# Attention and a two-layer MLP: load order of the second batch, first-layer groups ahead of its turns, and the engine that casts Q and K

## The chip, the cores and the metric

The kernel runs on one core of a Trainium2 chip. Its engines work side by side, each from its own queue, in the order in which the queue was written: TensorE (PE; its weight loads are shown as PEld), VectorE (DVE), ScalarE (ACT), GpSimd (POOL) and SyncE (SP), which here only issues DMAs. The metric is the device time of one execution in microseconds (us), as the median of several runs.

## The reference: what is computed

Sliding-window attention over 8 batches, 8 heads, 576 positions and 64 values a head, with a window of 32 to each side, and behind it a two-layer MLP with a squared ReLU on the 4608 tokens of 512 values. All inputs and the output are float32.

```python
scores = scale * np.matmul(q, k.transpose(0, 1, 3, 2))
mask = np.abs(pos[:, None] - pos[None, :]) <= window        # window = 32
scores = np.where(mask, scores, -1000000000.0)
attn = np.exp(scores - max);  attn = attn / (sum + 1e-09)
x = np.matmul(attn, v)  ->  (4608, 512)
h = x @ w_in                       # 512 -> 2048
r = np.maximum(h, 0.0)
out = (s * (r * r) + b) @ w_out    # 2048 -> 512
```

## The kernel before

**Two programs in one.** Attention makes columns of XT (x transposed, bf16, a ring of 2048 tokens). The MLP reads them in token blocks of 224, 128, 160, 256, 256 and then 512 tokens. The first three blocks (512 tokens, NE = 3) come from batch 0 alone. `s1(m, f0)` is the first layer: for a block m it multiplies with 128 columns of w_in at a time (or two or four such, in the small blocks), four matmuls each, into one of the two halves of the PSUM tile W; ScalarE applies the ReLU (L1131), VectorE squares (L1133) into GT. `s2` is the second layer: 16 matmuls for each 128 tokens into a half of the tile O (L1142), scaled and given the bias on VectorE (L1158) and stored (L1162). For the first three blocks `early` (L1173) does the second layer instead: 128 tokens have four accumulators (both halves of O and of AVN), and it goes through w_out in eight steps, as the pieces of w_out come in. Ahead of it, `colsum` sums w_out by columns for the bias (L1183, L1187, L1190, L1192); it needs all pieces of w_out and uses the second half of AVN, which `early` can use only after that.

**Attention of batches 0 and 1.** Q and K of a pair of heads are loaded as 128 x 512 float32 (`load_pair`, L667), cast to bf16 (`cast_qk`, L692: K on VectorE; Q of batch 1 on GpSimd), transposed on TensorE into a half of W (L705) and copied out (L710, L711); this is called the turn of a pair (`turn_pair`). Scores (L944), exponentials (L987), masks (L992), the product with V (L869), the division (L893, L895) and a transpose (L902, L910) follow. The last 64 positions go by themselves (`load_rest`, `turn_rest`).

**Attention of batches 2 to 7.** `piece` loads 512 positions of Q, 512 of K, and the last 64 of both, in this order, as float32 into two neighbouring staging buffers (L752), casts them in two halves x = 0, 1 (L760) by the engines in CASTE (one pair of engines for batch 2, one for the later ones), and has the halves transposed by DMA (L767) into QT and KTR. GpSimd copies KTR to KT (L777). Scores are at L811, exponentials at L839, masks at L843. The loads of a batch wait for the product with V of two batches before (`paced`). V comes by L582 and is cast at L591.

**Staging.** All loads of weights and of Q and K share a ring of 8 buffers (STG), taken in the order in which the kernel's text asks for them. A load waits until the cast that read its buffer last is done. The casts write a ring of 6 buffers (NAT).

**Order.** The kernel's text adds tasks to a graph (`_Graph.add`) with a cost, a key and what they read and write. `plan` then lists them: at each step the task that can start first by its own clock, and among equals that with the lowest key. The list is the order of each engine's queue. For a DMA, `dma=("l", units, cost)` gives the time on the shared rings by units times cost in ns; `ORDER1` gives the order in which SyncE loads what follows w_in: ("w", i) is a quarter of w_out in two pieces (L554, cast at L557), ("p", i) the pair i of batch 1, ("v", i) a V tile of batch 1, ("e", 0) its last positions. `FIRST` lists what the kernel's text asks for between `colsum` and `early`: (m, i) is the i-th quarter of the first layer of block m, TURN the turn and the scores of the next pair of batch 1. As turns and first-layer groups both use the halves of W, whatever stands earlier in FIRST uses such a half first; between other tasks the planner is free.

The turns of batch 1 have key -17.5 and up, a first-layer group of the first blocks this one:

```python
key = P1[m, f0] if m >= NE else -20.0 + f0 // 4 + 0.1 * m
```

Of the kernel before, what the change touches and what calls it, by code (L numbers as in the profile page):

```python
# [30 lines left out]
WINE = ("pool", "pool", "pool", "pool")  # L31
TURNKEY = -17.5
TURN = (None, 0)
FIRST = ((0, 0), (0, 1), (1, 0), (1, 1), (2, 0), (0, 2), (2, 1), (1, 2), (2, 2), (0, 3), TURN, TURN, (1, 3), TURN, (2, 3), TURN)
WOUTE = (("pool", "pool"),) * 4
TAIL = ("act", "dve")
HOST = (("k", 3), ("q", 0))
HELD = (2200.0, 1500.0, 1500.0, 1500.0)
OPEN = -24.4
REST = ("pool", "pool")  # L40
ORDER1 = (("w", 0), ("w", 1), ("w", 2), ("w", 3), ("p", 0), ("p", 1), ("p", 2), ("p", 3),
          ("v", 0), ("v", 1), ("e", 0), ("v", 2), ("v", 3), ("v", 4))
SWITCH = 215.0
XTS = 4000.0
ROWS = 4
# [2 lines left out]
PACE = ((-1, -1, -1),) * 3  # L48
CASTS = 40.0
LATE = 8  # L50
CASTE = (("pool", "pool"), ("pool", "dve"))
SLACK = (1000.0, 2000.0, 3000.0, 3000.0)
PACEV = ((-1,-1,0,0,1),(0,0,1,1,2),(0,0,1,1,2))
EV0 = ("dve", "act", "dve", "act", "dve")
# [27 lines left out]
class _Graph:  # L82
# [13 lines left out]
    def add(self, stream, fns, cost, reads=(), writes=(), key=0.0, accum=False, dma=None, waits=(),  # L96
            lat=None, slack=0.0):
        if not isinstance(fns, list):
            fns = [fns]
        after = [self.chain] if key < -100 and self.chain else []  # L100
        t = _Task(len(self.tasks), stream, fns, cost, self.LAT[stream] if lat is None else lat, key,
                  dma, slack, after)
        t.deps.update(waits)
        for a in after:
            assert a.stream == stream
            a.next.append(t)
        for r in reads:
            assert r in self.writer, r
            t.deps.add(self.writer[r])
        for w in writes:  # L110
            if w in self.writer:
                t.deps.add(self.writer[w])
            if not accum:
                t.deps.update(self.readers.get(w, ()))
        t.deps.discard(t)
        for r in reads:
            self.readers.setdefault(r, []).append(t)
        for w in writes:
            self.writer[w] = t
            if not accum:  # L120
                self.readers[w] = []
        self.tasks.append(t)
        if key < -100:
            self.chain = t
        return t
# [201 lines left out]
def bass_sliding_window_symmetric__then__act_starrelu_kernel(  # L327
# [23 lines left out]
    with ExitStack() as es:  # L351
# [184 lines left out]
        def pieces(lo, hi, step):  # L536
            return range(lo // step, (hi - 1) // step + 1)

        def take(what, n):
            ring[what] += 1  # L540
            return (ring[what] - 1) % n
# [26 lines left out]
        def late(b):  # L568

            return "sp" if b < LATE else "act"  # L570
# [166 lines left out]
        def q_later(b):  # L737
            return QTS[b % 2].rearrange("p (i a) s -> p i a s", i=4)

        def piece(b, parts, key, waits):  # L740


            slot = b % 2
            ring["stg"] += ring["stg"] % 2
            ring["nat"] += ring["nat"] % 2
            si, _ = take("stg", NSTG), take("stg", NSTG)
            ni, _ = take("nat", NNAT), take("nat", NNAT)
            stg = STGS[:, si:si + 2, :].rearrange("p x c -> p (x c)")
            nat = NATS[:, ni:ni + 2, :].rearrange("p x c -> p (x c)")
            stgr, natr = [("STG", si), ("STG", si + 1)], [("NAT", ni), ("NAT", ni + 1)]  # L750
            top = max(p0 + n // 4 for _, _, n, p0 in parts)
            add(late(b), [lambda e, name=name, t0=t0, n=n, p0=p0: e.dma_start(  # L752
                stg[p0:p0 + n // 4, :].rearrange("p (h c) -> p h c", h=H),
                src_of[name][b, :, t0:t0 + n, :].rearrange("h (p i) d -> p h (i d)", i=4))
                for name, t0, n, p0 in parts],
                500.0 * len(parts), writes=stgr, key=key - 20.0, waits=waits,
                dma=("l", sum(n for _, _, n, _ in parts) // 8, 68.0 if late(b) == "sp" else 61.0))
            for x in (0, 1):
                eng = CASTE[min(b, 3) - 2][x]
                add(eng, lambda e, x=x: e.tensor_copy(  # L760
                    nat[0:top, 1024 * x:1024 * x + 1024].rearrange("p (i h d) -> p h i d", h=H, i=2),
                    stg[0:top, :].rearrange("p (h i d) -> p h i d", h=H, i=4)[:, :, 2 * x:2 * x + 2, :]),
                    110 + (0.53 if eng == "dve" else 1.05) * 1024, reads=stgr, writes=[("NAT", ni + x)], key=key + CASTS, slack=SLACK[0])
            for name, t0, n, p0 in parts:
                np_, s0, xs = n // 4, t0 // 4, pieces(t0, t0 + n, 64)
                dst = q_later(b)[:, :, :, 16 + s0:16 + s0 + np_] if name == "q" else KTR[slot][:, :, :, s0:s0 + np_]
                add("sp", lambda e, dst=dst, p0=p0, np_=np_: e.dma_start(  # L767
                    dst.rearrange("p i a s -> p (i a) s"), nat[p0:p0 + np_, :], transpose=True),
                    2000.0 if n > 64 else 1200.0, reads=natr,
                    writes=[("QT", slot, x, pr) for x in xs for pr in range(NPAIR)] if name == "q" else [("KTR", slot, t0)],  # L770
                    key=key + 0.1, dma=("t", np_, 20.0))
                if name == "q":
                    continue
                land["kt", b, t0] = g.tasks[-1]
                for c in range(t0, t0 + n, 128):
                    w = min(128, t0 + n - c)
                    add("pool", lambda e, c=c, w=w: e.tensor_copy(  # L777
                        KT[slot][:, :, c:c + w].rearrange("p a (s i) -> p a s i", i=4),
                        KTR[slot][:, :, :, c // 4:(c + w) // 4].rearrange("p i a s -> p a s i")),
                        100 + 5.5 * w, reads=[("KTR", slot, t0)],  # L780
                        writes=[("KT", slot, x, pr) for x in pieces(c, c + w, 64) for pr in range(NPAIR)],
                        key=key + 3.0, slack=SLACK[1])

        def later(b, key):
            slot = b % 2
            if b < 4:
                for c0, x in ((0, 0), (160, WIN + S)):
                    add("pool", lambda e, c0=c0: e.memset(QTS[slot][:, :, c0:c0 + 16], 0.0), 400,
                        writes=[("QTZ", slot, x)] + [("QT", slot, x, pr) for x in range(NTILE) for pr in range(NPAIR)],
                        key=key - 20.0)  # L790
            for i, parts in enumerate(((("q", 0, 512, 0),), (("k", 0, 512, 0),), (("q", 512, 64, 0), ("k", 512, 64, 32)))):
                piece(b, parts, key + 0.01 * i, [paced(b, PACE[min(b, 4) - 2][i])] +
                      ([land["v", seq_of(b - 1), group_of(b - 1)[-1]]] if b > PAIRS or LATE == PAIRS else []))
# [230 lines left out]
        def attention():  # L1024
# [30 lines left out]
            for i, src in enumerate((moe_s, moe_b)):  # L1055
# [3 lines left out]
                reads=[("SROW", 0), ("SROW", 1)], writes=[("SB128", 0), ("SB128", 1)], key=P2[0] - 8.0, slack=500.0)  # L1059
            for step in ORDER1:  # L1060
                if step[0] == "w":
# [119 lines left out]
        def colsum():  # L1181

            add("pe", [lambda e, fc=fc, x=x: e.matmul(  # L1183
                AVN[32 * x:32 * x + 32, 1, 0:128], lhsT=ONESW[:, 0:32], rhs=WOUT_BF[:, fc, 128 * x:128 * x + 128],
                start=(fc == 0), stop=(fc == 15)) for fc in range(16) for x in range(4)],
                1100, reads=["ONESW"] + [("Wout", i, x) for i in range(4) for x in (0, 1)], writes=[("AVN", 1)], key=-12.0)
            add("dve", [lambda e, x=x: e.tensor_copy(block[32 * x:32 * x + 32, 128 * x:128 * x + 128],  # L1187
                                                     AVN[32 * x:32 * x + 32, 1, 0:128]) for x in range(4)],
                800, reads=[("AVN", 1)], writes=[("OUTS", NOUT - 1)], key=-12.0)
            add("pe", lambda e: e.matmul(AVN[:, 1, :], lhsT=even, rhs=block, start=True, stop=True),  # L1190
                950, reads=[("OUTS", NOUT - 2), ("OUTS", NOUT - 1)], writes=[("AVN", 1)], key=-12.0)
            add("dve", lambda e: e.tensor_scalar(CVEC[:, :], AVN[:, 1, :], SB128[:, 1:2], None, ALU.mult),  # L1192
                680, reads=[("AVN", 1), ("SB128", 1)], writes=[("CVEC", x) for x in (0, 1)], key=P2[0])
# [9 lines left out]
        colsum()  # L1203
        for m, i in FIRST:
            if m is None:
# [269 lines left out]
```

## Time and profile before

| | us |
|---|---|
| median of 3 runs | 315.75 (314.89 to 316.14) |
| the profiled execution | 317.31 |
| its span, first to last instruction | 315.5 |
| TensorE busy | 296.7 |
| VectorE busy | 195.5 |
| GpSimd busy | 93.0 |
| GpSimd casts of later Q, K (L760) | 21, of 1271 ns on average |
| VectorE casts of later Q, K (L760) | 15, of 740 ns on average |
| queued DMA, share of 16 engines' span | 75.5% |

The profile is of one execution. A row of a timeline gives the start and the length in us, the engine, the line, the operation, what is written from what, and in brackets the idle time of the engine ahead of it and what ended that. Neighbouring instructions of one kind are merged (x8). A row of the DMA-issuing queue (SPq) has the time from issue to the end of issuing, waiting included. The matmuls of TensorE are pipelined, so their rows overlap a little.

### The profile page before, as it was taken

The page shows a single profiled execution, that of the slowest core. Times are in us where ns is not written, and L with a number is a line of the kernel's source. Part 1 is how long each engine was busy: PE and PEld are TensorE (multiplying, and loading weights), DVE is VectorE, ACT ScalarE, POOL GpSimd, SP SyncE. Part 2 cuts the span into 40 slices and gives each one's busy share as a digit, 9 for nine tenths or more (in the row PEclk, how much of TensorE's full clock was granted, in tenths as well). Part 3 has the DMA queues.
Part 4 walks back from the last instruction along what each step waited for, and adds up shares of the span by engine and source line. Part 5 has one row for each costly group of instructions (what it writes and reads, how often), then busy time and mean ns, then how long its engine had stood idle before and what let it go on. Part 6 is the DMA issues. An engine that isn't in the chain of part 4 may idle for free.

```text
span 315.5 us, 7901 instructions
## 1 busy us (share of the span) xinstructions
PE 296.7 (94%) x3304; PEld 160.6 (51%) x3348; DVE 195.5 (62%) x387; ACT 141.9 (45%) x224; POOL 93.0 (29%) x110
## 2 busy tenths in 40 slices
PE   7788989999979998999999999999999999999996
PEld 3367756577734544544444444444444444444444
DVE  4678476876596777888577687766445543333312
ACT  4755425356525773654255346444444333333300
POOL 5468854671236235131613241260000000000000
PEclk9999999999999999999999999999999999999999
DMA  6999999997998998799999999996221110000022
GB/s 198 331 386 386 372 251 218 218 199 246 236 188 205 294 140 166 219 225 169 175 318 157 161 221 336 165 154 162 64 59 50 52 46 33 35 34 34 36 91 80
DMA packets 100055, 56.10 MB, mean 178 GB/s; under 512 B 72048, under 2 KB 91248, under 8 KB 100016
## 3 DMA queue, kind: packets, MB, share of 16 engines
q1 hardware_dynamic: 100016, 55.56, 75.5%
q8 instruction: 27, 0.44, 0.6%
q14 instruction: 12, 0.10, 0.1%
HBM read 36.70 MB, written 9.44 MB: 146 GB/s over the span
## 4 chain that ended last, share of the span: by engine, by line
PE 68%; DMA 19%; DVE 6%; issue 3%; SPq 2%; POOL 1%; ACT 0%; POOLq 0%
PE o L1142 30%; PE w L1124 28%; DMA stg<-in_k_dram 10%; DMA stg<-in_moe_w_out_dram 3%; PE avn L869 3%; DMA stg<-in_moe_w_in_dram 3%; DVE gt L1133 2%; PE avn L1173 2%; DMA stg<-in_q_dram 2%; PE sc L811 1%; PE o L1173 1%; DMA vst<-in_v_dram 1%; SPq L667 1%; DVE xn L895 1%; DVE nat L760 1%
## 5 line engine op out<-in xcount | busy, mean ns | idle before, releaser
L1124 PE MATMUL w<-xt,win 128*128 128x512 bf16 (+4 forms) x749 | 140.2, 324 | 3.0 <-ACT r L1131 1.4
L1131 ACT ACTIVATE r<-w 128x512 bf16<-128x512 f32 (+2 forms) x148 | 86.6, 586 | 107.1 <-PE w L1124 91.3
L1142 PE MATMUL o<-wout,gt 128*128 128x512 bf16 (+1 forms) x510 | 123.1, 372 | 2.0 <-issue 1.4
L1133 DVE TENSOR_TENSOR gt<-r 128x512 bf16<-128x512 bf16 (+2 forms) x148 | 79.9, 545 | 72.3 <-ACT r L1131 71.9
L1124 PEld LDWEIGHTS w<-xt,win 128*128 128x128 bf16 x768 | 68.3, 98 | 54.0 <-DVE kt L711 0.9
L1142 PEld LDWEIGHTS o<-wout,gt 128*128 128x128 bf16 x528 | 50.6, 98 | 54.6
L760 POOL CAST nat<-stg 128x1024 bf16<-128x1024 f32 (+1 forms) x21 | 26.7, 1271 | 60.7 <-DMA stg<-in_q_dram 37.6
L777 POOL COPY kt<-ktr 128x512 bf16<-128x512 bf16 (+1 forms) x30 | 31.6, 1054 | 38.5 <-DMA ktr<-nat 37.1
L839 ACT ACTIVATE ex<-sc 128x1024 bf16<-128x1024 f32 (+1 forms) x28 | 28.7, 1023 | 23.2 <-PE avn L869 22.4
L1158 DVE SCALAR_TENSOR_TENSOR outs<-o,sb,cvec 128x512 f32<-128x512 f32 (+1 forms) x35 | 25.4, 729 | 14.2 <-PE o L1142 14.0
L895 DVE TENSOR_TENSOR xn<-avn,rec 128x512 bf16<-128x512 f32 (+1 forms) x31 | 21.4, 689 | 1.1 <-DVE rec L893 0.2
L843 DVE TENSOR_TENSOR ex<-ex,mask 128x1024 bf16<-128x1024 bf16 (+1 forms) x28 | 21.2, 758 | 1.0 <-ACT ex L839 0.2
L869 PE MATMUL avn<-vb,ex 64*64 64x65 bf16 x944 | 19.9, 197 | 1.5 <-issue 1.3
L869 PEld LDWEIGHTS avn<-vb,ex 64*64 64x64 bf16 x944 | 12.9, 106 | 14.5 <-issue 8.7
L760 DVE CAST nat<-stg 128x1024 bf16<-128x1024 f32 (+1 forms) x15 | 11.1, 740 | 7.2 <-DMA stg<-in_k_dram 5.1
L591 DVE CAST vb<-vst 128x512 bf16<-128x512 f32 (+1 forms) x28 | 13.7, 494 | 0.0
L811 PE MATMUL sc<-qt,kt 64*64 64x128 bf16 x432 | 11.3, 216 | 0.0
L910 ACT COPY xt<-avn 128x512 bf16<-128x512 bf16 (+2 forms) x14 | 7.1, 516 | 8.1 <-PE avn L902 8.1
L893 DVE RECIPROCAL rec<-avn 128x8 f32<-128x8 f32 (+1 forms) x31 | 6.2, 201 | 5.9 <-PE avn L869 5.5
L557 POOL CAST win<-stg 128x1024 bf16<-128x1024 f32 x8 | 8.4, 1056 | 3.7 <-DMA stg<-in_moe_w_in_dram 3.6
L557 POOL CAST wout<-stg 128x1024 bf16<-128x1024 f32 x8 | 9.0, 1122 | 1.7 <-DMA stg<-in_moe_w_out_dram 1.0
L1173 PE MATMUL o<-wout,gt 128*128 128x512 bf16 x29 | 8.2, 379 | 1.0 <-POOL wout L557 0.9
(119 smaller groups left out, 146.1 us busy)
## 6 DMA issues: line engine op xcount, KB each, us to landing
out_dram<-outs SPq DMA_DIRECT2D x35, 256.0 KB, 2.5
vst<-in_v_dram SPq DMA_DIRECT2D x28, 256.0 KB, 5.2
stg<-in_k_dram SPq DMA_DIRECT2D x6, 1024.0 KB, 11.1
stg<-in_q_dram SPq DMA_DIRECT2D x6, 1024.0 KB, 6.6
stg<-in_moe_w_in_dram SPq DMA_DIRECT2D x8, 512.0 KB, 9.2
stg<-in_moe_w_out_dram SPq DMA_DIRECT2D x8, 512.0 KB, 9.6
stg<-in_q_dram SPq DMA_DIRECT2D x8, 256.0 KB, 5.4
stg<-in_k_dram SPq DMA_DIRECT2D x8, 256.0 KB, 5.4
```

Of the source, the lines that this page charges most:

```text
L760: add(eng, lambda e, x=x: e.tensor_copy(nat[0:top, 1024 * x:1024 * x + 1024].rearrange("p (i h d) -> p h i d", h=H, i=2), stg[0:top, :].re ...
L777: add("pool", lambda e, c=c, w=w: e.tensor_copy(KT[slot][:, :, c:c + w].rearrange("p a (s i) -> p a s i", i=4), KTR[slot][:, :, :, c // 4: ...
L839: add("act", lambda e, dst=flat_dst, src=flat_src: e.activation(dst, src, AF.Exp, bias=0.0, scale=0.125), 190 + 0.833 * 512 * len(hs), rea ...
L843: add("dve", lambda e, flat=flat, mask=mask: e.tensor_tensor(flat, flat, mask, ALU.mult), 130 + 0.53 * 512 * len(hs), reads=[("E", ei, hp, ...
L869: return [lambda e: e.matmul(av[64 * x:64 * x + 64, h, 0:D + 1], lhsT=buf[64 * g:64 * g + 64, h % 2, h // 2, c:c + 64], rhs=VB[64 * g:64 * ...
L895: add("dve", lambda e: e.tensor_tensor(XN[xi][0:p1, :].rearrange("p (a c) -> p a c", a=H), av[0:p1, :, 0:D], REC[ri][0:p1, :].rearrange("p ...
L1124: add("pe", [lambda e, g=g, kc=kc: e.matmul(wt[:, g, :], lhsT=WIN_BF[:, kc, (f0 + g) * 128:(f0 + g + 1) * 128], rhs=XT[:, kc, t0 % XR:t0 % ...
L1131: add("act", lambda e: e.activation(rt, wt, AF.Relu, bias=0.0, scale=1.0), 190 + 0.833 * ng * nt, reads=[("W", wb)], writes=[("R1", rb)], ...
L1133: add("dve", lambda e: e.tensor_tensor(GT[gs][:, f0:f0 + ng, g0:g0 + nt], rt, rt, ALU.mult), 130 + 0.53 * ng * nt, reads=[("R1", rb)], wri ...
L1142: add("pe", [lambda e, fc=fc: e.matmul(O[:, ob, 0:cn], lhsT=GT[gs][:, fc, g0:g0 + 128], rhs=WOUT_BF[:, fc, c0:c0 + cn], start=(fc == 0), s ...
L1158: add("dve", lambda e: e.scalar_tensor_tensor(OUTS[us][:, 0:cn], bank, SB128[:, 0:1], CVEC[:, c0:c0 + cn], ALU.mult, ALU.add), 200 + 1.07 ...
L1173: add("pe", [lambda e, fc=fc, bank=bank, gs=gs, g0=g0: e.matmul(bank, lhsT=GT[gs][:, fc, g0:g0 + 128], rhs=WOUT_BF[:, fc, :], start=(fc == ...
```

## The change

Four constants change. The loads of batch 1 and w_out come in the order pairs 0 and 1, first half of w_out, pairs 2 and 3, second half of w_out (before: w_out, then the pairs). In FIRST, the last two first-layer groups stand ahead of all turns (before: between them). From batch 3 on, GpSimd casts both halves of each piece (before: the second half on VectorE). And the planner counts 74 instead of 68 ns a unit for loads of the later Q and K.

```diff
-FIRST = ((0, 0), (0, 1), (1, 0), (1, 1), (2, 0), (0, 2), (2, 1), (1, 2), (2, 2), (0, 3), TURN, TURN, (1, 3), TURN, (2, 3), TURN)
+FIRST = ((0, 0), (0, 1), (1, 0), (1, 1), (2, 0), (0, 2), (2, 1), (1, 2), (2, 2), (0, 3), (1, 3), (2, 3), TURN, TURN, TURN, TURN)
...
-ORDER1 = (("w", 0), ("w", 1), ("w", 2), ("w", 3), ("p", 0), ("p", 1), ("p", 2), ("p", 3),
-          ("v", 0), ("v", 1), ("e", 0), ("v", 2), ("v", 3), ("v", 4))
+ORDER1 = (("p", 0), ("p", 1), ("w", 0), ("w", 1), ("p", 2), ("p", 3), ("w", 2), ("w", 3), ("v", 0), ("v", 1), ("e", 0), ("v", 2), ("v", 3), ("v", 4))
...
-CASTE = (("pool", "pool"), ("pool", "dve"))
+CASTE = (("pool", "pool"), ("pool", "pool"))
...
                 500.0 * len(parts), writes=stgr, key=key - 20.0, waits=waits,
-                dma=("l", sum(n for _, _, n, _ in parts) // 8, 68.0 if late(b) == "sp" else 61.0))
+                dma=("l", sum(n for _, _, n, _ in parts) // 8, 74.0 if late(b) == "sp" else 61.0))
             for x in (0, 1):
                 eng = CASTE[min(b, 3) - 2][x]
                 add(eng, lambda e, x=x: e.tensor_copy(
...
```

## The prediction, made before the changed kernel was run

> **What bounds the kernel now.** I read the page's first lines, then the table of busy time by stretch, then TensorE's instructions in order of time with the idle time ahead of each, and last the other queues around its gaps.
>
> ```profile
> span 315.5 us, 7901 instructions
> PE 296.7 (94%) x3304; PEld 160.6 (51%) x3348; DVE 195.5 (62%) x387; ACT 141.9 (45%) x224; POOL 93.0 (29%) x110
> ...
> 20.00:30.00 10.00, 9.07 (x156) 7.98 (x156) 8.70 (x15) 6.18 (x12) 8.57 (x10) 1.00 1.05 386
> 30.00:40.00 10.00, 8.76 (x86) 6.89 (x88) 4.67 (x9) 3.94 (x8) 8.36 (x8) 1.00 1.07 372
> 40.00:50.00 10.00, 9.34 (x162) 6.36 (x164) 7.48 (x17) 3.73 (x7) 4.85 (x7) 1.00 1.02 232
> ...
> 80.00:90.00 10.00, 8.52 (x148) 5.77 (x148) 6.71 (x11) 4.88 (x8) 4.49 (x3) 1.00 1.16 224
> ...
> 100.00:120.00 20.00, 18.07 (x245) 9.34 (x240) 16.04 (x31) 14.14 (x23) 7.34 (x6) 1.00 1.04 230
> ...
> 220.00:260.00 40.00, 39.14 (x373) 18.82 (x377) 20.13 (x43) 16.33 (x26) 0.00 (x0) 1.00 0.19 56
> ```
>
> Columns after the stretch and its length are busy time of PE, PEld, DVE, ACT and POOL, then granted clock, DMA share and GB/s. TensorE is the bound: busy 296.7 of 315.5 us at full clock, and in the last third, where nothing else is scarce, 39.14 of 40. Its idle time is all that a change of order can win: 315.5 - 296.7 = 18.8 us, of which the ramp and the tail, which the change leaves alone, hold a good part. Between 20 and 120 us it gathers in few places: 30 to 40 (1.24 us), 80 to 90 (1.48), 100 to 120 (1.93). Four single gaps make most of it:
>
> ```profile
> 30.27 0.38 PE L1173 MATMUL o<-wout,gt 128*128 128x512 bf16 x1 [0.93 <-POOL wout L557]
> ...
> 40.24 0.40 PE L705 MATMUL w<-ident,nat 128*128 128x128 bf16 x4 [1.16 <-DVE nat L692]
> ...
> 88.77 0.32 PE L869 MATMUL avn<-vb,ex 64*64 64x65 bf16 x16 [1.27 <-issue]
> ...
> 119.42 0.40 PE L902 MATMUL avn<-ident,xn 128*128 128x128 bf16 x4 [1.30 <-DVE xn L895]
> ```
>
> 0.93 + 1.16 = 2.09 us come from the loads of w_out and of batch 1's heads; 1.27 + 1.30 = 2.57 us from something on VectorE. The ceiling of this change is thus near 4.7 us.
>
> **Part 1, the loads and the first-layer groups.** SyncE's queue serves loads in order, and DMA is full there (share 1.05 to 1.07), so I read landings from the casts that waited for them.
>
> ```profile
> 27.41 1.16 POOL L557 CAST win<-stg 128x1024 bf16<-128x1024 f32 x1 [0.31 <-DMA stg<-in_moe_w_in_dram]
> 28.76 3.78 POOL L557 CAST wout<-stg 128x1024 bf16<-128x1024 f32 x3 [0.18 <-DMA stg<-in_moe_w_out_dram]
> ...
> 38.19 1.04 POOL L557 CAST wout<-stg 128x1024 bf16<-128x1024 f32 x1 [0.31 <-DMA stg<-in_moe_w_out_dram]
> ...
> 40.38 0.62 POOL L692 CAST nat<-stg 128x512 bf16<-128x512 f32 x1 [0.48 <-DMA stg<-in_q_dram]
> ...
> 43.36 0.61 POOL L692 CAST nat<-stg 128x512 bf16<-128x512 f32 x1 [0.89 <-DMA stg<-in_q_dram]
> ```
>
> Eight w_out pieces land from 28.76 to 38.19, so 9.43 / 7 = 1.35 us each. From one Q of a pair to the Q two pairs on (40.38 to 43.36) four loads land: 0.75 us each. After the last w_in piece at 27.41 the new order then gives, as an estimate from these rows: pairs 0 and 1 by 30.4; four w_out pieces by 35.8; pairs 2 and 3 by 38.8; the last four w_out pieces by 44.2 instead of 38.2. The bytes are the same, and the loads of V behind them come when they did. The staging ring allows it: pairs 0 and 1 take buffers 0 to 3, the first w_out pieces 4 to 7, and pairs 2 and 3 come back to 0 to 3, which the casts of pairs 0 and 1 free at about 31, well ahead of their turn.
>
> ```profile
> 20.64 0.94 PE L1124 MATMUL w<-xt,win 128*128 128x224 bf16 x8
> ...
> 22.60 1.70 PE L1124 MATMUL w<-xt,win 128*128 128x224 bf16 x16
> ...
> 24.45 4.90 PE L1124 MATMUL w<-xt,win 128*128 128x224 bf16 x64
> ...
> 40.57 1.08 PE L1183 MATMUL avn<-wout,onesw 128*32 128x128 bf16 x64
> ...
> 46.84 0.81 PE L1173 MATMUL avn<-wout,gt 128*128 128x512 bf16 x3 [0.16 <-issue]
> ...
> 53.56 0.86 PE o L1173 x4
> ```
>
> What can TensorE do meanwhile? The twelve first-layer groups are 192 matmuls; 8 + 16 + 64 = 88 are done by 29.3. The 104 left, at 4.90 / 64 = 0.077 us each, are 8.0 us and need no load any more. They now stand ahead of the turns, so they fill 29.3 to 37.3, past the place where TensorE waited 0.93 us for w_out. At 37.3 the first half of w_out and pairs 0 and 1 are there: 24 second-layer matmuls into three banks, at 0.86 / 4 = 0.216 us each (the last row, from the chain that ended last), are 5.2 us, the turns and scores of four pairs some 3 us more, until about 45.5. The last w_out piece, cast for about 1.1 us, is ready at 45.3. So the 1.16 us wait for a turn also has cover, but with nothing to spare. What is late next: the column sum of w_out, at 40.57 before, needs all eight pieces, so it moves to about 45.5, and from it to the first use of the fourth bank it took 46.84 - 40.57 = 6.27 us; that bank opens at about 51.8 instead. Until then the second half of w_out gives three banks another 5.2 us of work, plus the last scores. That is cover to about 51, a microsecond short.
>
> Bounds: all of 2.09 us won; or, if the last w_out pieces come into an empty queue and the column sum holds its bank back, some 2 us lost. I take 1.2 us won: two waits gone, less the microsecond by which the cover is short.
>
> **Part 2, the casts.** Fifteen halves go from VectorE to GpSimd.
>
> ```profile
> L760 POOL CAST nat<-stg x21: 1032/1210/1578, 57.4 to 200.0; 128x1024 bf16<-128x1024 f32 x14, 48x1024 bf16<-48x1024 f32 x7
> L760 DVE CAST nat<-stg x15: 676/685/1519, 81.2 to 201.5; 128x1024 bf16<-128x1024 f32 x10, 48x1024 bf16<-48x1024 f32 x5
> ...
> 83.99 0.69 DVE L895 TENSOR_TENSOR xn<-avn,rec 128x512 bf16<-128x512 f32 x1
> 86.53 0.69 DVE L760 CAST nat<-stg 128x1024 bf16<-128x1024 f32 x1 [1.85 <-DMA stg<-in_k_dram]
> 87.14 1.52 DVE L843 TENSOR_TENSOR ex<-ex,mask 128x1024 bf16<-128x1024 bf16 x1
> ...
> 108.89 0.69 DVE L760 CAST nat<-stg 128x1024 bf16<-128x1024 f32 x1 [1.12 <-DMA stg<-in_q_dram]
> ...
> 112.45 0.42 DVE L1133 TENSOR_TENSOR gt<-r 128x512 bf16<-128x512 bf16 x1
> 114.55 0.69 DVE L760 CAST nat<-stg 128x1024 bf16<-128x1024 f32 x1 [1.69 <-DMA stg<-in_k_dram]
> 115.16 1.26 DVE L1133 TENSOR_TENSOR gt<-r 128x512 bf16<-128x512 bf16 x1
> 116.34 1.52 DVE L760 CAST nat<-stg 48x1024 bf16<-48x1024 f32 x1
> ...
> 118.67 0.69 DVE L895 TENSOR_TENSOR xn<-avn,rec 128x512 bf16<-128x512 f32 x1
> ```
>
> This is what the two gaps of 2.57 us are. VectorE's queue is in order. At 84.7 it stands at the cast of a K load that lands at 86.5; the mask of the exponentials behind it then runs until 88.66, and TensorE starts the product with V at 88.77. At 112.9 the same: it waits 1.69 us for K, casts twice, and the normalised rows that TensorE waits for end at 119.36. With no cast of a load on VectorE these waits stand on GpSimd, where only casts and K copies are queued. Gain: 2.57 less the 0.16 us that such a change of operands shows anyway (the 46.84 row), twice: 2.25 us. Bounds: 2.57, and nothing.
>
> The cost: GpSimd does both halves in turn, at 1.21 us (median) for the second one, 15 x 1.21 = 18 us on an engine busy 93.0 of 315.5. Behind the casts stand the transposes in SyncE's queue and the K copies.
>
> ```profile
> 82.13 5.22 SPq L1162 DMA_DIRECT2D out_dram<-outs  x1
> ...
> 89.08 2.91 SPq L767 DMA_TRANSPOSE qt<-nat  x1
> 92.10 3.04 SPq L767 DMA_TRANSPOSE ktr<-nat  x1
> ...
> 97.54 5.69 POOL L777 COPY kt<-ktr 128x512 bf16<-128x512 bf16 x5 [7.97 <-DMA ktr<-nat]
> ...
> 99.75 0.24 PE L811 MATMUL sc<-qt,kt 64*64 64x128 bf16 x1
> ...
> 56.50:65.00 8.50, 8.05 (x163) 5.11 (x163) 7.08 (x15) 2.57 (x5) 7.03 (x8) 1.00 1.07 231
> ```
>
> For batch 3, K lands at 86.5, two GpSimd casts end by 89.0, and its transpose left at 92.10 anyway, because SyncE stood 5.22 us at a store that VectorE owed. So the later half costs nothing as long as SyncE is the later one; without that cover it is 1.21 us for each of five batches, against a margin of 99.75 - (97.54 + 5.69 / 5) = 1.07 us. Batch 2 already casts everything on GpSimd, and in its stretch (56.5 to 65) TensorE idles 0.45 us of 8.5.
>
> What speaks against it stands in the same rows: a square that takes 0.42 us alone takes 1.26 at 115.16, beside a GpSimd cast. One more such delay per moved cast is 15 x 0.84 = 12.6 us on VectorE, more than the 15 x 0.685 = 10.3 us taken from it. I still count it as nothing, since four buffers lie between squares and their readers, but it is a rival below.
>
> The Trainium skill ("SBUF — State Buffer", Who interferes with whom) says that a VectorE instruction with two SBUF inputs and a GpSimd one that reads SBUF exclude one another for a whole instruction. The 1.26 us row agrees. By that rule alone the sum would have no VectorE gain in it and would come to rival C.
>
> **Part 3, the planner's 74 for 68.** It moves no instruction by itself; the planned landing of a full piece (64 units) comes 64 x 6 = 384 ns later, so casts, transposes and scores are placed behind more MLP work. Q landed at 108.9 and K at 114.55, 5.6 us for one piece, so later is nearer to the truth. Counted at nothing: TensorE has MLP work to put first until the end. Were a score to come so late that a block's rows are missing, the cost is at most 0.4 us a piece.
>
> **Sum.** -1.2 - 2.25 = -3.45 us. The profiled execution took 317.31 us (span 315.5), 1.56 above the median of 315.75; it becomes 313.86, and the median 312.3.
>
> **Rivals.** A is the forecast, 312.3 (its own range 310.9 to 313.9).
> B: the loads win nothing, because the column sum and the last w_out pieces take the waits over. For it: the cover above ends a microsecond short. Against: 8.0 us of groups free of loads. Casts alone: 315.75 - 2.25 = 313.5.
> C: the casts win nothing: GpSimd's second cast holds VectorE by 0.84 us where it stood for a load before, so masks and normalised rows come as late. For: the 1.26 and 1.52 us rows. Against: batch 2's stretch. 315.75 - 1.2 = 314.55. The same time comes out if the planner puts new waits where the old ones were.
> D, slower: K arrives late. GpSimd's two extra casts of K and of the short piece (2 x 1.21 = 2.42 us) both come before the first K copy, and TensorE's score stands in order ahead of MLP work. Price: (2.42 - 1.07) x 5 batches = 6.8 us; with the gains, 315.75 + 6.8 - 3.45 = 319.1. It decides from a lateness of 1.07 + 3.45 / 5 = 1.76 us a batch on. Against: SyncE's cover of 3 us, and a planner that knows of the longer cast and puts the scores later.
>
> **Chances.** A 0.48, B 0.15, C 0.20, D 0.17. Half a per cent, 1.6 us, is about what can be told from no change: faster (below 314.2) is A and most of B, 0.60; no change is C with the edges of the others, 0.22; slower (above 317.3) 0.18. The range reaches down to all of 4.7 us and a little of the smaller waits, 310.4, and up to a D that is two thirds paid, 318.0.
>
> **What would show it.** Right: first-layer groups dense from 29 to 37 us with no wait for w_out; no VectorE cast behind a K load after 60 us; no gap over 0.5 us at 80 to 90 and 100 to 120; idle in 20 to 120 us down by some 3.5. Wrong: a wait for w_out or for the column sum's bank between 42 and 52; scores (L811) preceded by idle time that ends with GpSimd's K copy; squares of 1.26 us ahead of every TensorE gap; or a TensorE that is late at 220 us by as much as it is at the end.

## The result, and the profile after

| | before | after |
|---|---|---|
| median of 22 runs each, us | 315.02 | 313.36 |
| lowest and highest | 313.77 to 318.06 | 312.42 to 317.73 |
| ratio after / before, 95% interval | | 0.994 (0.9919 to 0.996) |
| the profiled execution | 317.31 | 312.42 |

The change wins 0.6%, some 1.9 us. Ratios here leave disturbed executions out; the medians beside them do not. The two profiled executions differ by 4.9 us, far more: the one of before is among its slowest, the one of after its fastest. So these two traces show where waits stood, but not what they are worth in the median; that took more traces of before.

The page of the changed kernel, then its table of busy time by stretch (columns as before):

```profile
span 310.6 us, 7883 instructions
PE 295.3 (95%) x3305; PEld 160.3 (52%) x3348; DVE 191.8 (62%) x372; ACT 142.3 (46%) x224; POOL 106.8 (34%) x125
...
L1132 DVE TENSOR_TENSOR gt<-r 128x512 bf16<-128x512 bf16 (+2 forms) x148 | 87.1, 601 | 69.2 <-ACT r L1130 68.5
...
L759 POOL CAST nat<-stg 128x1024 bf16<-128x1024 f32 (+1 forms) x36 | 41.1, 1140 | 51.2 <-DMA stg<-in_q_dram 38.2
```

```profile
20.00:30.00 10.00, 9.80 (x156) 9.10 (x156) 6.24 (x15) 6.60 (x13) 6.59 (x7) 1.00 1.06 374
30.00:40.00 10.00, 9.42 (x108) 7.74 (x108) 6.14 (x11) 4.66 (x11) 6.80 (x8) 1.00 1.07 374
40.00:50.00 10.00, 9.25 (x160) 5.35 (x159) 8.94 (x18) 5.11 (x8) 7.23 (x9) 1.00 1.04 251
...
80.00:90.00 10.00, 9.79 (x150) 5.89 (x151) 6.95 (x12) 4.95 (x7) 5.70 (x6) 1.00 1.23 204
...
100.00:120.00 20.00, 19.33 (x228) 9.78 (x230) 17.01 (x30) 11.74 (x20) 9.33 (x9) 1.00 1.06 206
```

(Line numbers are one lower from here on, as the diff takes a line out.) TensorE's idle time fell from 0.93 to 0.20 us at 20 to 30, from 1.24 to 0.58 at 30 to 40, from 1.48 to 0.21 at 80 to 90 and from 1.93 to 0.67 at 100 to 120. It grew a little at 40 to 50 (0.66 to 0.75). Some of this idle time is not real, and the last section comes back to it. All four gaps that the prediction named are gone, and two smaller ones have come. GpSimd's 36 casts took 41.1 us, at a mean of 1140 ns (1271 before). TensorE's timeline of after:

```profile
23.87 7.92 PE L1123 MATMUL w<-xt,win 128*128 128x224 bf16 x104
32.28 0.38 PE L1172 MATMUL o<-wout,gt 128*128 128x512 bf16 x1 [0.48 <-POOL wout L556]
...
44.48 1.08 PE L1182 MATMUL avn<-wout,onesw 128*32 128x128 bf16 x64 [0.53 <-POOL wout L556]
```

The first-layer groups do run on without a load: 104 matmuls in one piece where before there were 64. But the planner still asked for w_out in the middle of them, 0.48 us early, and for the column sum ahead of the last w_out cast, 0.53 us early. GpSimd's queue gives the landings that the prediction had worked out:

```profile
30.96 1.04 POOL L556 CAST wout<-stg 128x1024 bf16<-128x1024 f32 x1 [3.20 <-DMA stg<-in_moe_w_out_dram]
...
35.15 1.04 POOL L556 CAST wout<-stg 128x1024 bf16<-128x1024 f32 x1 [0.52 <-DMA stg<-in_moe_w_out_dram]
...
39.29 1.06 POOL L556 CAST wout<-stg 128x1024 bf16<-128x1024 f32 x1 [0.99 <-DMA stg<-in_moe_w_out_dram]
...
43.39 1.04 POOL L556 CAST wout<-stg 128x1024 bf16<-128x1024 f32 x1 [0.25 <-DMA stg<-in_moe_w_out_dram]
```

The fourth piece starts its cast at 35.15 (35.8 was estimated for its landing), the last at 43.39 (44.2).

**Three stretches.** To compare traces whose start-up differs by up to 1.2 us, I cut each at three of TensorE's rows: the first first-layer group, the first group of block 3 (which needs batch 1), and the last merged run of the second layer. For before and after:

```profile
61.94 1.92 PE L1124 MATMUL w<-xt,win 128*128 128x256 bf16 x16
...
297.50 14.88 PE L1142 MATMUL o<-wout,gt 128*128 128x512 bf16 x83
```

```profile
20.20 0.94 PE L1123 MATMUL w<-xt,win 128*128 128x224 bf16 x8
...
59.93 1.92 PE L1123 MATMUL w<-xt,win 128*128 128x256 bf16 x16
...
292.64 14.88 PE L1141 MATMUL o<-wout,gt 128*128 128x512 bf16 x83
```

Early: 61.94 - 20.64 = 41.30 us before, 59.93 - 20.20 = 39.73 after. Middle: 297.50 - 61.94 = 235.56 before, 232.71 after. The rest, 18.00 and 17.96, is the same in all traces to 0.4 us. The experiments below are read by these two numbers beside their times.

### The profile page after: what moved, and what is told of

The parts are those of the page before. It is cut to its first block, busy times and chain, and to the rows that moved or that the text cites. A ratio compares the mean times of both kernels' runs of the same rounds, so it can differ in the third digit from the quotient of the medians.

```text
span 310.6 us, 7883 instructions
## 1 busy us (share of the span) xinstructions
PE 295.3 (95%) x3305; PEld 160.3 (52%) x3348; DVE 191.8 (62%) x372; ACT 142.3 (46%) x224; POOL 106.8 (34%) x125
## 4 chain that ended last, share of the span: by engine, by line
PE 78%; DMA 12%; SPq 3%; issue 2%; POOL 2%; DVE 2%; ACT 0%; POOLq 0%
PE o L1141 35%; PE w L1123 32%; DMA stg<-in_moe_w_out_dram 5%; PE avn L868 4%; DMA stg<-in_moe_w_in_dram 3%; DMA stg<-in_k_dram 3%; PE sc L810 2%; PE avn L1172 2%; DMA stg<-in_v_dram 1%; DVE gt L1132 1%; SPq L666 1%; PE o L1172 1%; POOL wout L556 1%; SPq L677 1%; PE avn L901 1%
## 5 line engine op out<-in xcount | busy, mean ns | idle before, releaser
L1123 PE MATMUL w<-xt,win 128*128 128x512 bf16 (+4 forms) x750 | 138.2, 325 | 2.9 <-ACT r L1130 1.6
L1132 DVE TENSOR_TENSOR gt<-r 128x512 bf16<-128x512 bf16 (+2 forms) x148 | 87.1, 601 | 69.2 <-ACT r L1130 68.5
L1141 PE MATMUL o<-wout,gt 128*128 128x512 bf16 (+1 forms) x508 | 120.6, 372 | 2.4 <-issue 1.6
L759 POOL CAST nat<-stg 128x1024 bf16<-128x1024 f32 (+1 forms) x36 | 41.1, 1140 | 51.2 <-DMA stg<-in_q_dram 38.2
L776 POOL COPY kt<-ktr 128x512 bf16<-128x512 bf16 (+1 forms) x30 | 30.8, 1028 | 36.0 <-DMA ktr<-nat 34.5
L842 DVE TENSOR_TENSOR ex<-ex,mask 128x1024 bf16<-128x1024 bf16 (+1 forms) x28 | 19.8, 708 | 1.2 <-ACT ex L838 0.5
L590 DVE CAST vb<-vst 128x512 bf16<-128x512 f32 (+1 forms) x28 | 12.3, 445 | 1.1 <-DMA vst<-in_v_dram 1.1
L986 ACT ACTIVATE ex<-sc 128x1024 bf16<-128x1024 f32 (+2 forms) x7 | 6.2, 902 | 5.0 <-PE sc L943 5.0
## 6 DMA issues: line engine op xcount, KB each, us to landing
stg<-in_k_dram SPq DMA_DIRECT2D x6, 1024.0 KB, 10.4
```

Of the source, the lines that this page charges most:

```text
L759: add(eng, lambda e, x=x: e.tensor_copy(nat[0:top, 1024 * x:1024 * x + 1024].rearrange("p (i h d) -> p h i d", h=H, i=2), stg[0:top, :].re ...
L776: add("pool", lambda e, c=c, w=w: e.tensor_copy(KT[slot][:, :, c:c + w].rearrange("p a (s i) -> p a s i", i=4), KTR[slot][:, :, :, c // 4: ...
L842: add("dve", lambda e, flat=flat, mask=mask: e.tensor_tensor(flat, flat, mask, ALU.mult), 130 + 0.53 * 512 * len(hs), reads=[("E", ei, hp, ...
L1123: add("pe", [lambda e, g=g, kc=kc: e.matmul(wt[:, g, :], lhsT=WIN_BF[:, kc, (f0 + g) * 128:(f0 + g + 1) * 128], rhs=XT[:, kc, t0 % XR:t0 % ...
L1132: add("dve", lambda e: e.tensor_tensor(GT[gs][:, f0:f0 + ng, g0:g0 + nt], rt, rt, ALU.mult), 130 + 0.53 * ng * nt, reads=[("R1", rb)], wri ...
L1141: add("pe", [lambda e, fc=fc: e.matmul(O[:, ob, 0:cn], lhsT=GT[gs][:, fc, g0:g0 + 128], rhs=WOUT_BF[:, fc, c0:c0 + cn], start=(fc == 0), s ...
```

## The experiments

| run | loads | groups | casts | cost | ratio (95%) | traced, us | early | middle |
|---|---|---|---|---|---|---|---|---|
| first trace of before | old | old | old | 68 | | 317.31 | 41.30 | 235.56 |
| c1_before_again | old | old | old | 68 | | 316.16 | 41.17 | 233.89 |
| c3_before_third | old | old | old | 68 | | 314.47 | 41.10 | 232.84 |
| c4_before_fourth | old | old | old | 68 | | 317.08 | 41.07 | 235.67 |
| e1_loads | new | new | old | 68 | 1.0009 (0.9978 to 1.0041) | 319.02 | 40.66 | 237.20 |
| e2_casts | old | old | new | 68 | 0.9999 (0.9964 to 1.0034) | 318.18 | 41.16 | 236.44 |
| e3_cost | old | old | old | 74 | 1.0 (0.9976 to 1.0023) | 314.93 | 40.34 | 233.35 |
| e4_loads_casts | new | new | new | 68 | 0.9969 (0.9938 to 1.0001) | 314.61 | 40.23 | 233.61 |
| e5_loads_cost | new | new | old | 74 | 0.9958 (0.9931 to 0.9984) | 313.8 | 40.01 | 233.07 |
| e6_casts_cost | old | old | new | 74 | 0.9992 (0.9968 to 1.0016) | 314.36 | 41.04 | 233.20 |
| e7_order_casts_cost | new | old | new | 74 | 1.0007 (0.9983 to 1.0031) | 316.3 | 42.86 | 232.57 |
| the change, first trace | new | new | new | 74 | 0.994 (0.9919 to 0.996) | 312.42 | 39.73 | 232.71 |
| c2_after_again | new | new | new | 74 | 0.994 (0.9914 to 0.9966) | 314.43 | 40.82 | 232.78 |
| e8_held | new | new | new | 74 | 0.9982 (0.9941 to 1.0023) | 312.81 | 39.97 | 232.75 |

The table has all eight combinations of three parts: loads and groups, casts, cost. With the old loads and groups, nothing moves the ratio: 0.9999, 1.0 and 0.9992 for casts, cost and both. With the new ones it is 1.0009 alone, 0.9969 with the casts, 0.9958 with the cost and 0.994 with both. So the loads win only together with another part, and the other parts only together with the loads. Neighbours among these four have intervals that overlap; those of the first and the last lie apart.

The middle stretch sorts by the cost: 232.57 to 233.35 us in the seven traces with 74, 232.84 to 237.20 in the seven with 68. The third trace of before is thus as short there as those of the changed kernel. The sizes are those of single executions: three of the seven with 74 are the fastest of their kernel (the first of the change, e6, e8).

### The kernel before, three more times

No edit.

> The kernel before, unchanged, for a second trace. The first one belongs to an execution of 317.31 us, while the median of all is 315.02. If the four gaps are a fixed consequence of the written order, they are here again, each within 0.3 us (0.93, 1.16, 1.27, 1.30), and the 2.3 us of difference lie elsewhere. If they depend on when loads happen to land, at least one of the two VectorE gaps (1.27, 1.30) is below 0.6 us here, and the changed kernel can win less from them in the median than the first trace showed.

> The kernel before, a third trace. The forecast's sum took 2.57 us for two VectorE gaps out of a trace of 317.31 us; the second trace (316.16 us) had one of 0.98. Theory G (these gaps belong to slower executions, where K lands later against VectorE's queue): in an execution near the median of 315.4 or below, they sum to under 1 us. Rival: they sum to 1 us or more whatever the time.

> As the run ahead of it, a fourth trace: by theory G the time above 313.5 us of span goes with the sum of the VectorE gaps; by the rival the gaps are of one size and the times differ by the start, the granted clock or gaps elsewhere.

The two early gaps came back each time. In the order of the runs, TensorE's gaps over 0.3 us from 29 us on:

```profile
31.00 0.38 PE L1173 MATMUL o<-wout,gt 128*128 128x512 bf16 x1 [1.05 <-POOL wout L557]
41.01 0.40 PE L705 MATMUL w<-ident,nat 128*128 128x128 bf16 x4 [1.21 <-DVE nat L692]
89.09 0.32 PE L869 MATMUL avn<-vb,ex 64*64 64x65 bf16 x16 [0.98 <-issue]
```

```profile
29.77 0.60 PE L1173 MATMUL o<-wout,gt 128*128 128x512 bf16 x2 [0.53 <-POOL wout L557]
40.04 0.40 PE L705 MATMUL w<-ident,nat 128*128 128x128 bf16 x4 [1.24 <-DVE nat L692]
```

```profile
29.91 0.60 PE L1173 MATMUL o<-wout,gt 128*128 128x512 bf16 x2 [0.64 <-POOL wout L557]
40.12 0.40 PE L705 MATMUL w<-ident,nat 128*128 128x128 bf16 x4 [1.18 <-DVE nat L692]
88.13 0.32 PE L869 MATMUL avn<-vb,ex 64*64 64x65 bf16 x16 [0.81 <-issue]
102.11 0.34 PE L902 MATMUL avn<-ident,xn 96*128 96x96 bf16 x4 [0.53 <-DVE xn L895]
143.88 0.32 PE L869 MATMUL avn<-vb,ex 64*64 64x65 bf16 x16 [1.38 <-DVE ex L843]
```

The 0.53 us in the fourth trace has another cause. No cast of a load stands ahead of it; two squares do, which took 2.29 us beside GpSimd's K copies (0.42 us is one square alone):

```profile
98.92 2.29 DVE L1133 TENSOR_TENSOR gt<-r 128x512 bf16<-128x512 bf16 x2 [0.74 <-ACT r L1131]
```

```profile
96.37 5.32 POOL L777 COPY kt<-ktr 128x512 bf16<-128x512 bf16 x5 [7.44 <-DMA ktr<-nat]
```

With the first trace, the gaps behind VectorE's waits for loads sum to 2.57, 0.98, 0 and 0.81 + 1.38 = 2.19 us, for executions of 317.31, 316.16, 314.47 and 317.08 us. Take the sum away and 314.5 to 315.2 us are left each time. Four traces are few, but they fit theory G: the early gaps belong to the written order, these VectorE gaps to how late K happens to land, and an execution near the median has little of them. The second trace shows the one that failed to come. GpSimd's cast of its half of K starts at 112.26, so K had landed while VectorE was still busy:

```profile
112.26 1.07 POOL L760 CAST nat<-stg 128x1024 bf16<-128x1024 f32 x1 [3.87 <-DMA stg<-in_k_dram]
```

```profile
112.35 1.26 DVE L1133 TENSOR_TENSOR gt<-r 128x512 bf16<-128x512 bf16 x1
113.53 0.68 DVE L760 CAST nat<-stg 128x1024 bf16<-128x1024 f32 x1
```

VectorE's K cast at 113.53 has no idle time ahead of it; in the first trace it had 1.69 us. What makes K land earlier or later from one execution to the next was not found.

### Each part alone

```diff
 e1_loads: ORDER1 and FIRST as in the change
 e2_casts:
-CASTE = (("pool", "pool"), ("pool", "dve"))
+CASTE = (("pool", "pool"), ("pool", "pool"))
 e3_cost:
-68.0 if late(b) == "sp"
+74.0 if late(b) == "sp"
```

> New load order and the first-layer groups ahead of the turns; casts and planner cost as before. Theory A (both parts pay): 1.2 us less than before, ratio 0.996, TensorE's idle time from 20 to 60 us down from 3.3 to about 2, and the gaps behind VectorE's casts still there between 80 and 120. Rival B (the column sum and the last w_out pieces take the waits over): ratio 1.000, idle from 20 to 60 unchanged, a gap of 1 us or more between 42 and 52.

> GpSimd casts all later Q, K; loads, groups and planner cost as before. Theory A: 2.25 us less at most, ratio 0.993 to 0.996, no gap over 0.5 us between 80 and 120. Rival C (GpSimd's casts hold VectorE's two-input operations by 0.84 us each, and the gaps come back): ratio 0.999 to 1.002, with squares of 1.2 us ahead of the gaps. Rival D (K late): ratio above 1.005, idle time ahead of scores that GpSimd's K copy ends.

> Only the planner's 74 for 68. Counted at nothing in the forecast: ratio 0.999 to 1.001 with the VectorE gaps where they were. If instead the planner's later landing alone places masks and products behind the wait, so that VectorE's wait for K delays nobody, the gaps at 80 to 120 go without any cast moved and the ratio is 0.993 to 0.997.

None wins anything that can be measured. The casts alone do take the VectorE gaps away, and K is late in their place (the prediction's rival D). TensorE's gaps in that trace, and GpSimd around the largest:

```profile
122.78 0.32 PE L869 MATMUL avn<-vb,ex 64*64 64x65 bf16 x16 [0.65 <-POOL kt L777]
151.04 0.32 PE L869 MATMUL avn<-vb,ex 64*64 64x65 bf16 x16 [0.66 <-POOL kt L777]
181.28 0.32 PE L869 MATMUL avn<-vb,ex 64*64 64x65 bf16 x16 [2.12 <-POOL kt L777]
```

```profile
180.20 4.79 POOL L777 COPY kt<-ktr 128x512 bf16<-128x512 bf16 x4 [5.63 <-DMA ktr<-nat]
```

The product with V and the scores are written into TensorE's queue as one step (`pe_part`), so the product waits for K too: the first copy ends near 181.2, and TensorE starts at 181.28. 0.65 + 0.66 + 2.12 = 3.43 us is more than VectorE's gaps took in any trace of before.

The loads alone shortened the early stretch to 40.66, but their trace fell on an execution whose granted clock was 0.83 between 80 and 90 us. It has a gap of 3.09 us there, with VectorE 3.77 us at a load of Q. I take no price from it. But the twelve times of this kernel do not speak for the loads alone either: their median is 316.86 us, with 315.40 before, and the longest, 319.47, had a mean granted clock of 1.0. That the gap at the load of Q is the reason was seen in this one trace only. The cost alone left no gap at 88 or 119 us, as its second expectation said, but one of 0.68 us at 96.8 (for a ScalarE copy), and its ratio is the first expectation's, 1.0.

### Parts in pairs, and the whole again

> The whole change without the planner's 74. With casts alone the VectorE gap at 88 went, but three new gaps (0.65, 0.66, 2.12 us) stood ahead of scores and products that waited for GpSimd's K copy. Theory E (the moved casts need the later planned landing): those gaps of 0.6 us or more are here again between 110 and 200, 2 to 4 us in all, and the ratio is 0.997 to 1.002. Rival: the K waits came from the old load order; then there are none here, and the ratio is 0.992 to 0.996, as for the whole change.

> The whole change without the moved casts. With loads alone the VectorE gap grew to 3.09 us at 86.8, as TensorE came earlier to a K load that did not; with the cost alone it was gone. Theory E (the later planned landing is what takes that gap away): no gap over 0.7 us between 80 and 120, early idle as in the whole change, ratio 0.993 to 0.997, so the casts are worth little in it. Rival (the moved casts take the gap away): a gap of 1 to 3 us at 84 to 90 and a ratio of 0.998 to 1.003.

> Casts and the planner's 74, with the old load order and groups. Theory E: no wait for K copies between 110 and 200 and no VectorE gap at 80 to 120; the early gaps (0.8 and 1.2 us) stay; ratio 0.994 to 0.998. Rival (the planner's 74 does not cover the longer casts): K gaps of 0.6 us and more, ratio 0.999 to 1.003.

> The whole change once more, for a second trace and time beside its parts on one chip. Ratio 0.992 to 0.996. If the idle time of 20 to 300 us decides (7.2 us in the first trace, 11.1 and 10.1 in the two of before), it is between 7 and 9 us here, with no gap above 0.7 us.

Theory E holds in part. Without the 74, one K wait is back with the moved casts (e4_loads_casts), 1.13 us where it expected 2 to 4 in all:

```profile
179.53 0.32 PE L868 MATMUL avn<-vb,ex 64*64 64x65 bf16 x16 [1.13 <-POOL kt L776]
```

With the 74 and the casts (e6_casts_cost) the 3.43 us of K waits are gone, as theory E had it, but the ratio is its rival's: 0.9992, not 0.994 to 0.998. The copies of the same batch start earlier and the score later:

```profile
177.37 5.42 POOL L777 COPY kt<-ktr 128x512 bf16<-128x512 bf16 x5 [7.60 <-DMA ktr<-nat]
182.58 0.32 PE L869 MATMUL avn<-vb,ex 64*64 64x65 bf16 x16
```

First copy near 178.5, product and score at 182.58: 4 us to spare in this trace. And with the loads, the cost alone already keeps the middle at 233.07 us (e5_loads_cost). So the moved casts are worth little once the planner places masks and products later: 0.9958 without them, 0.994 with them, and the intervals overlap. In the second trace of the whole change (c2_after_again) a K wait of 0.34 us is left, at 100.23, and its wait for w_out is 0.96 us, above the 0.7 that was expected at most. What the pairs do settle is the early part. With casts and cost both in, the loads and groups take the ratio from 0.9992 to 0.994, 0.5% or 1.6 us, and the intervals just do not overlap.

### The groups put back between the turns

```diff
 e7_order_casts_cost: the whole change, but
-FIRST = (..., (0, 3), (1, 3), (2, 3), TURN, TURN, TURN, TURN)
+FIRST = (..., (0, 3), TURN, TURN, (1, 3), TURN, (2, 3), TURN)
```

> The whole change, but with the first-layer groups between the turns as before. If the groups ahead of the turns carry the early gain, the early gaps come back (about 1 us more idle between 20 and 60 than the 2.0 to 2.8 of the whole change) and the ratio is 0.997 to 1.001. If the load order alone carries it, the ratio is that of the whole change, 0.992 to 0.996.

The whole gain goes: 1.0007, and the early stretch is the longest of all, 42.86 us. TensorE and VectorE there:

```profile
43.06 0.40 PE L704 MATMUL w<-ident,nat 128*128 128x128 bf16 x4 [2.05 <-DVE kt L710]
```

```profile
40.54 0.41 DVE L691 CAST nat<-stg 128x512 bf16<-128x512 f32 x1
40.88 1.52 DVE L1132 TENSOR_TENSOR gt<-r 128x448 bf16<-128x448 bf16 x2
42.33 0.68 DVE L710 COPY kt<-w 128x512 bf16<-128x512 bf16 x1
```

The third transpose (K of pair 1) needs a half of W, which VectorE empties at 42.33 to 43.01, behind casts and squares. The last two groups, which could have filled this, stand behind that transpose in the same halves of W and cannot go first. The new load order pays only with the groups ahead.

### The last wait, for the column sum

```diff
 e8_held: the whole change, and
-HELD = (2200.0, 1500.0, 1500.0, 1500.0)
+HELD = (3200.0, 1500.0, 1500.0, 2500.0)
```

> The whole change, with the planner told that the last quarter of w_out is usable 1000 ns later and the first quarter too (HELD 3200 and 2500 for 2200 and 1500). In every trace with the new load order TensorE waits 0.5 to 1.0 us for the last cast of w_out ahead of the column sum. Expected: that gap below 0.3 us, 0.3 to 0.6 us less than the whole change, ratio 0.991 to 0.995. If the wait only moves (to the bank that the column sum holds, or to the turns), the ratio stays at 0.994.

In its trace (311.0 us of span) the wait ahead of the column sum is gone, the one for the first w_out piece (0.56 us) is not. Its 12 times fall in two groups, eight at 312.8 to 314.6 and four at 316.8 to 318.0, and the ratio is no better than the change's. The two groups differ in the granted clock: 0.972 or 0.973 on average in the four, 0.999 or 1.0 in the eight. The one execution of the change at 0.972 is its longest too, 317.73 us. The median of the eight is 313.99 us, 0.996 of the 315.22 before, so what was gained ahead of the column sum does not show in the time. No kernel measured here is clearly faster than the change.

## Why the prediction was right, step by step

The time came out as forecast in sign, and 313.36 us lies in the range; the forecast was 312.3, a gain of 3.45 us against about 1.9. The range of 310.4 to 318.0 also held no change at all. By time the forecast is off by 1.1 us, by gain by some 1.6: it started from 315.75 us, and the median of before turned out as 315.02.

The sum adds parts that do not add: alone, each of the three is worth nothing that can be measured (1.0009, 0.9999, 1.0). And one sign came true by luck. TensorE's idle time from 20 to 120 us fell by 4.0 us between the first two traces, where some 3.5 were forecast, but the first of them was among the slowest executions of before, and the second was the fastest of after. The third trace of before and the second of after took the same time (314.47 and 314.43 us) and idle 2.96 and 3.35 us there.

- **Part 1, loads and groups, 1.2 us: right in size, for a part that pays only beside the others.** Landings came as worked out. The fill ran without a load from 24 to 32 us, not to 37. The early stretch averages 41.03 us in the seven traces with the old loads and groups (the four of before, e2, e3, e6) and 40.29 in the five with both new (the change twice, e1, e4, e5): 0.74 us by the traces, 1.6 by the ratios of e6 and the change. One trace of each set had a granted clock of 0.66 or 0.67 from 10 to 15 us (e3, e5), and no wait for w_out above 0.3 us after it; without these two the difference is 0.78. Not worked out: the wait for w_out stayed, at 0.48 us, since the planner put a w_out step among the groups; and TensorE waited for the column sum's own input rather than for its bank. That the loads pay only with the groups ahead was not foreseen either.
- **Part 2, the casts, 2.25 us: the term that was mis-sized.** The mechanism is as described: VectorE's queue stood at a K load, masks and rows behind it came late, and the two gaps are gone. The price was read off one slow execution. The four traces of before show 0 to 2.57 us for it. With the old loads, casts and cost together win 0.25 us by ratio (0.9992), well inside the interval. In the whole change, what is left of the 1.9 us after the 0.74 of the early stretch is 1.15 us for everything after 60 us, casts and cost together; with the 1.6 of the ratios it is 0.3. How it divides between the two is open. The 0.16 us taken off twice was no wait (below).
- **Part 3, the cost, counted at nothing: right alone (1.0), wrong in the sum.** The casts need it. With the casts moved it took the traced middle stretch from 236.44 (e2) to 233.20 us (e6), and with the loads but without the casts from 237.20 (e1) to 233.07 (e5). These are single traces, and e2's and e1's executions lie above the medians of their kernels, e6's is its fastest; by ratio the cost is worth 0.9999 to 0.9992 beside the casts and 1.0009 to 0.9958 beside the loads, with intervals that overlap in both pairs.
- **Rival D, K late.** Its place was right: three waits for K copies in e2_casts, 3.43 us against 6.8 worked out. In the whole change 0.34 us of it is left at most, as the 74 puts the scores later.
- **Rival C, GpSimd against VectorE.** The delay is there, and in the changed kernel off the path. The 148 squares took 76.5 to 79.9 us in the four traces of before and 77.8 to 87.1 us in the seven with the casts moved, 78.7 and 83.3 on average, so some 4.6 of the 10.4 to 13.4 us of casts taken off VectorE came back. No gap of TensorE over 0.5 us in the changed kernel stands behind it; in the kernel before one did, 0.53 us in the fourth trace. The Trainium skill ("SBUF — State Buffer", Who interferes with whom) would have a square, with its two SBUF inputs, and a GpSimd operation that reads SBUF exclude one another; the square of 1.26 us beside a GpSimd cast, against 0.42 alone, agrees with it.

## What to carry to other kernels

Before a gap in a trace is priced, see where that execution stands among the times, and trace it again if it stands at the edge. Here the wait for a turn came back in all seven traces with the old order (1.16 to 1.26 us), while the gaps behind VectorE's loads came and went (0 to 2.57 us). Parts of a change need not add up: before their prices are summed, ask what each is worth without the others. Moving a cast off an engine whose queue stands at a load only helped here once the planner knew the slower path; else the wait came back one step later. And the load order paid only where the work that was to fill its waits did not stand behind what waits, in the same buffer.

## What the runs showed that was not expected

The many idle times of 0.16 us in the first traces are no waits. Where they stand, a merged row has 7 or 3 matmuls instead of 8 or 4 (the 46.84 row of the prediction has three of four), and the page counts fewer matmuls than weight loads, x3304 against x3348. The second trace of after has all of them:

```profile
PE 301.8 (97%) x3348; PEld 160.5 (51%) x3348; DVE 186.0 (59%) x372; ACT 142.2 (45%) x224; POOL 106.6 (34%) x125
```

There no 0.16 us gap is left, TensorE's busy time is 301.8 us instead of 295.3, and the idle time from 20 to 300 us is 3.4 us instead of 7.2, although its true waits are the longer ones (0.96 us for w_out against 0.48). So 43 missing records in the first trace of after, and 44 in that of before, had been read as some 7 us of idle TensorE (44 x 0.16), more than all the waits that this change could remove; the prediction's 18.8 us of idle time held them too. The third trace of before has all records as well, and idles 3.0 us from 20 to 300. Idle sums are comparable only between traces with the same number of records.
